# Output projection of 14 of 16 blocks: eight quarter products replaced by seven products of sums, in a fused attention and gated-FFN kernel

## The chip, the cores and the metric

One core of one Trainium2 chip. The metric is device time in microseconds (us) of the whole program, best read from runs in the fast state. Engines are named as in the profile: PE is TensorE (matmuls), PEld its weight loads, DVE is VectorE, ACT is ScalarE, POOL is GpSimd, SP the queue that issues the output transfers.

## The reference, cut to what matters

```python
# attention with projected K and V, 8 batches x 8 heads x 1024 x 64 (all fp32)
k_proj = einsum('ks,bhsd->bhkd', E, k);  v_proj = einsum('ks,bhsd->bhkd', F, v)
attn_out = softmax(q @ k_proj.T / 8) @ v_proj
x = attn_out.transpose(0, 2, 1, 3).reshape(8192, 512)
# gated FFN, d_model 512, d_ff 1536
gate = 1 / (1 + exp(-(x @ w_gate)));  val = x @ w_val
out = (gate * val) @ w_out            # [8192, 1536] @ [1536, 512]
```

The last line is the output projection. The kernel handles 16 blocks of 512 tokens, two for each batch.

## The kernel before

Everything is laid out so that TensorE never rests. A gate step makes 128 of the 1536 hidden features of a block: four matmuls for the gate and four for the value (512 columns each), a tanh on ScalarE and one product on VectorE into `hT` (bf16, features on partitions). The projection of the block before is slotted in between, one tile of 128 tokens at a time. Attention of the next batch runs in the gaps of ScalarE, VectorE and GpSimd.

```python
KV = [sbuf(f"KV{i}", [P, H, S // P * DH], BF16) for i in range(3)]    # K and V, three buffers
rrow = sbuf("rrow", [P, 4, 512], FP32)                                # reciprocal rows
FB, AB = (0, 1, 2, 3), (4, 5, 6, 7)      # four PSUM banks for the FFN, four for attention

def mstep(blk, m):                       # a gate step: 8 matmuls of 512 columns
    pbs = {n: ffn.next() for n in "GV"}
    ...
    gate(blk, m, pbs["G"], pbs["V"])     # ACT: tanh; DVE: hT[blk % 2][:, m, :]

def oproj(blk, tt, pb, cols=((0, DM),)):                # 128 tokens of a block
    ...
        for m in range(NF):                              # 12 matmuls of 512 columns
            mm(pb, bank[pb][:, 0 : c1 - c0],
               hT[blk % 2][:, m, tt * P : (tt + 1) * P], wO[:, m, c0:c1], ...)
        dve(... o = 0.5 * bank ...)                      # eviction
        add("SP", ... out_v[blk // 2, t] <- o ...)
# schedule: after gate steps 2, 5, 8 and 11 of a block, one tile of the block before
gaps = {2: [0], 5: [1], 8: [2], 11: [3]}
```

(Cuts are marked with dots; block 0 and the last block have their four tiles in a row.)

The softmax here doesn't subtract the row's maximum and nothing guards it: scores larger than these inputs give would overflow.

## Time and profile before

| | before |
|---|---|
| median, before the prediction | 562.15 us (561.75 to 563.31, 3 runs) |
| TensorE busy | 550.6 of 559.7 us |
| VectorE / ScalarE busy | 257.0 / 199.6 us |
| TensorE's waits after the first load | 0.3 and 0.2 us |

How to read it: with one engine at 98%, no waits and a chain of work that stays on it, the shares of the other engines matter only where they could be late. The time can fall by giving TensorE less to do. The lines stand in the prediction.

### The profile page before, as it was taken

What the parts mean: (1) busy time and instruction counts of PE and PEld (TensorE: products, weight loads), DVE (VectorE), ACT (ScalarE), POOL (GpSimd) and SP (SyncE); (2) the same over time, 40 slices, a digit from 0 to 9 for tenths busy, and PEclk for the clock granted to TensorE, in tenths of its full rate; (3) what the DMA queues carried; (4) which work ended last, traced back from release to release, by engine and by line L of the source; (5) the groups of instructions that cost most, each with busy time, mean ns of one, the idle gap of its engine ahead of it and who ended that gap; (6) DMA issues with size and microseconds to landing.
All of it is one profiled execution on the core that took longest, in us unless ns stands there. A gap on an engine that the chain in (4) does not pass through costs nothing.

```text
span 559.7 us, 7742 instructions
## 1 busy us (share of the span) xinstructions
PE 550.6 (98%) x3057; PEld 249.4 (45%) x3057; DVE 257.0 (46%) x397; ACT 199.6 (36%) x358; POOL 113.2 (20%) x148
## 2 busy tenths in 40 slices
PE   5999999999999999999999999999999999999998
PEld 4544444444444444444444444444444444444444
DVE  4645363235733564344733456335553357433332
ACT  3563813533253422533226422345224422222220
POOL 9210201003700270004500063000900026000000
DMA  9999997924491359105591158802401101110012
GB/s 176 198 200 195 174 224 156 202 68 95 92 215 45 76 100 213 50 27 117 101 191 38 29 115 133 168 20 49 102 32 38 39 22 39 37 39 31 26 37 95
DMA packets 76564, 56.01 MB, mean 100 GB/s; under 512 B 34704, under 2 KB 68240, under 8 KB 76528
## 3 DMA queue, kind: packets, MB, share of 16 engines
q0 software_dynamic: 33984, 29.89, 34.5%
q1 hardware_dynamic: 42544, 25.63, 17.4%
q8 instruction: 24, 0.39, 0.3%
q14 instruction: 12, 0.10, 0.1%
HBM read 60.29 MB, written 16.78 MB: 138 GB/s over the span
## 4 chain that ended last, share of the span: by engine, by line
PE 98%; DMA 1%; DVE 1%; ACT 0%; issue 0%; SPq 0%
PE pF L221 92%; PE pA L221 6%; DMA EF<-in_F_dram 1%; DVE rden L596 0%; DVE xT L645 0%; DVE hT L1056 0%; ACT qT L225 0%; SPq L307 0%; DVE vpD L498 0%; DVE ost L1087 0%; ACT kp L225 0%
## 5 line engine op out<-in xcount | busy, mean ns | idle before, releaser
L225 ACT ACTIVATE sig<-pF 128x512 f32<-128x512 f32 x192 | 115.6, 602 | 297.2 <-PE pF L221 289.8
L1056 DVE SCALAR_TENSOR_TENSOR hT<-sig,pF 128x512 bf16<-128x512 f32 x192 | 131.6, 686 | 167.9 <-PE pF L221 129.4
L221 PE MATMUL pF<-xT,wV 128*128 128x512 bf16 x768 | 197.9, 379 | 0.3 <-DVE hT L1056 0.3
L221 PE MATMUL pF<-xT,wG 128*128 128x512 bf16 x768 | 198.0, 379 | 0.1
L221 PE MATMUL pF<-wO,hT 128*128 128x512 bf16 (+1 forms) x780 | 175.3, 376 | 0.0
L890 POOL PARTITION_BROADCAST rb<-rrow x96 | 76.9, 862 | 287.0 <-DMA rrow<-rden 281.9
L221 PEld LDWEIGHTS pF<-wO,hT 128*128 128x128 bf16 x780 | 75.3, 98 | 91.1 <-issue 2.5
L221 PEld LDWEIGHTS pF<-xT,wV 128*128 128x128 bf16 x768 | 75.0, 98 | 90.9 <-DVE hT L1056 1.0
L221 PEld LDWEIGHTS pF<-xT,wG 128*128 128x128 bf16 x768 | 73.0, 98 | 93.8 <-issue 7.1
L1087 DVE TENSOR_SCALAR ost<-pF 128x512 f32<-128x512 f32 (+1 forms) x65 | 44.4, 684 | 109.4 <-PE pF L221 109.4
L920 DVE TENSOR_TENSOR xT<-xu,rb 128x512 bf16<-128x512 f32 x48 | 39.2, 858 | 0.0
L816 DVE RECIPROCAL rden<-pA 128x128 f32<-128x128 f32 x26 | 24.6, 950 | 12.7 <-PE pA L221 12.7
L225 ACT ACTIVATE xu<-pA 128x512 f32<-128x512 f32 x46 | 24.5, 616 | 1.1 <-PE pA L221 1.1
L225 ACT ACTIVATE eT<-pF 128x512 bf16<-128x512 f32 x29 | 15.8, 595 | 22.9 <-PE pF L221 22.7
L225 ACT ACTIVATE eT<-pA 128x512 bf16<-128x512 f32 x35 | 19.3, 625 | 1.0 <-PE pA L221 1.0
L221 PE MATMUL pA<-KV,EFT 128*64 128x512 bf16 (+2 forms) x168 | 15.5, 323 | 0.0
L239 POOL DMA_DIRECT2D KV<-in_k_dram x9 | 8.0, 885 | 34.4 <-PE pF L221 34.4
L239 POOL DMA_DIRECT2D Qb<-in_q_dram x11 | 9.4, 865 | 14.7 <-PE pF L221 14.7
L221 PEld LDWEIGHTS pA<-KV,EFT 128*64 128x64 bf16 x168 | 8.0, 109 | 6.9 <-issue 2.9
L225 ACT ACTIVATE vpD<-pA 64x512 bf16<-64x512 f32 (+2 forms) x20 | 9.7, 485 | 1.0 <-PE pA L221 0.5
L225 ACT ACTIVATE xu<-pF 128x512 f32<-128x512 f32 x14 | 7.6, 594 | 3.7 <-PE pF L221 3.7
L221 PE MATMUL pA<-eT,vpD 64*64 64x512 bf16 (+1 forms) x112 | 8.4, 351 | 0.0
(78 smaller groups left out, 119.4 us busy)
## 6 DMA issues: line engine op xcount, KB each, us to landing
out_dram<-ost SPq DMA_DIRECT2D x63, 256.0 KB, 2.0
Qb<-in_q_dram POOLq DMA_DIRECT2D x7, 1024.0 KB, 19.8
KV<-in_k_dram POOLq DMA_DIRECT2D x7, 1024.0 KB, 9.8
KV<-in_v_dram POOLq DMA_DIRECT2D x7, 1024.0 KB, 14.9
wO<-in_moe_w_out_dram POOLq DMA_DIRECT2D x1, 1536.0 KB, 12.5
wG<-in_moe_w_gate_dram POOLq DMA_DIRECT2D x5, 256.0 KB, 17.7
wV<-in_moe_w_val_dram POOLq DMA_DIRECT2D x5, 256.0 KB, 18.3
KV<-in_k_dram POOLq DMA_DIRECT2D x2, 512.0 KB, 7.2
```

The source lines that it names most:

```text
L221: return add("PE", lambda e: e.matmul(o, lhsT, rhs, **kw), r=r, x=[("bank", b)])
L225: return add("ACT", lambda e: e.activation(o, i, func, scale=scale), r=r, w=w, x=x)
L239: add("POOL", lambda e: e.dma_start(o, i), r=r, w=w, dma=sem)
L816: lambda e: e.reciprocal(rden[:, cc], bank[bk][:, cc]),
L890: lambda e, n=n, i=2 * rnd + c, j=j, parts=parts: e.partition_broadcast(rb[0:parts, n, :], rrow[32 * j : 32 * j + 1, i, :], channels=parts),
L920: lambda e: e.tensor_tensor(xT[s][:, r, :, 256 * g : 256 * g + 256], xu[:, n, :].rearrange("p (f c) -> p f c", f=2), y.rearrange("p (f c) ...
L1056: lambda e: e.scalar_tensor_tensor(hT[blk % 2][:, m, :], sg[:, :], 1.0, bank[pv][:, :], ALU.add, ALU.mult,),
L1087: lambda e, pb=pb, c0=c0, c1=c1: e.tensor_scalar(o[:, c0:c1], bank[pb][:, 0 : c1 - c0], 0.5, None, op0=ALU.mult),
```

## The change

A block's projection is A·B, with A the tokens by features and B the weights. Cut both into quarters: the token halves and feature halves of A, the feature halves and column halves of B. Four result quarters need eight quarter products. Winograd's form of Strassen's scheme needs seven, with sums: S1 = A21 + A22, S2 = S1 - A11, S3 = A11 - A21, S4 = A12 - S2 of the activations, and T1 to T4 of the weights, made once. The sums after the products are made in PSUM: one bank runs P1, then P1 + S2·T2, then + S3·T3, then + A22·T4; on the way ScalarE takes a snapshot three times, and VectorE adds a snapshot when it evicts the other bank.

```diff
+        def s_sums(blk, n, ms):                       # n = 1..4, three feature tiles at a time
+            o, a, b, op, r, w = {
+                1: (S1, A21, A22, ALU.add, "A21 A22", "S1"),
+                2: (S2, S1, A11, ALU.subtract, "S1 A11", "S2"),
+                3: (A21, A11, A21, ALU.subtract, "A11 A21", "A21"),    # in place
+                4: (A12, A12, S2, ALU.subtract, "A12 S2", "A12"),      # in place
+            }[n]
+            dve(lambda e: e.tensor_tensor(o, a, b, op), ...)
+        def first_products(blk):
+            a, c = ffn.next(), ffn.next()
+            product(blk, a, "A11", "B11", True)       # 12 matmuls of 256 columns
+            keep_snap(0, a)                           # ACT reads bank a
+            product(blk, c, "A12", "B21", True, True)
+            add_snap(0, c, 0, 0)                      # DVE: bank c + snapshot -> out tile
+            for ms in ((0, 3), (3, 6)):
+                s_sums(blk, 4, ms)
+            product(blk, a, "S2", "T2")
+            keep_snap(1, a)
+            product(blk, c, "S1", "T1", True)
+            product(blk, a, "A21", "T3")
+            keep_snap(2, a)
+            add_snap(2, c, 1, 1)
+        def last_products(blk):
+            product(blk, a, "A22", "T4", stop=True)
+            act(o, bank[a] ..., scale=0.5)
+            product(blk, c, "A12", "B22", stop=True)
+            add_snap(1, c, 0, 1)
 ...
-                    gaps = {2: [0], 5: [1], 8: [2], 11: [3]}
+                    if blk >= 2 and m[-1] == 3:
+                        todo.append(lambda blk=blk: first_products(blk - 1))
+                    if blk >= 2 and m[-1] == 4:
+                        todo.append(lambda blk=blk: last_products(blk - 1))
 ...
-        KV = [... for i in range(3)]
+        KV = [... for i in range(2)]
-        rrow = sbuf("rrow", [P, 4, 512], FP32)
+        rrow = (eT[:, :, :] ... .bitcast(FP32) ...)   # room for the sums: rows now lie over eT
 ...
-                spots = (3, 4, 6, 7, 12, 13, 14, 15, 15, 21, 23, 25, 27)
+                spots = (7, 8, 10, 11, 13, 14, 15, 16, 16, 20, 22, 24, 25)   # attention's places
```

The first three sums of a block stand behind its gate steps 9 to 11 and behind steps 0 to 2 of the next block; the fourth stands among the products. Below, a round is the work between one batch's first score matmuls and the next one's, two blocks long; the odd block is the second of a batch, in which the next batch's attention puts most of its work on VectorE. One gate step (step 4) stands between the fifth and the sixth product.

More of the change, by code (lines that the diff above doesn't have):

```diff
@@ L160, in bass_linformer_attn__then__ffn_glu_sigmoid_kernel @@
         Qb = sbuf("Qb", [P, H, S // P * DH], BF16)
-        KV = [sbuf(f"KV{i}", [P, H, S // P * DH], BF16) for i in range(3)]
+        KV = [sbuf(f"KV{i}", [P, H, S // P * DH], BF16) for i in range(2)]
         kp = sbuf("kp", [P, NR, DH], BF16)
@@ L170, in bass_linformer_attn__then__ffn_glu_sigmoid_kernel @@
         rhl = sbuf("rhl", [P, 512], BF16)
-        rrow = sbuf("rrow", [P, 4, 512], FP32)
+        rrow = (
+            eT[:, :, :].rearrange("p n c -> p (n c)").bitcast(FP32)
+            .rearrange("p (i c) -> p i c", i=4)
+        )
         rb = sbuf("rb", [P, 8, 512], FP32)
@@ L180, in bass_linformer_attn__then__ffn_glu_sigmoid_kernel @@
         hT = [sbuf(f"hT{i}", [P, NF, 512], BF16) for i in range(2)]
-        ost = [sbuf(f"ost{i}", [P, DM], FP32) for i in range(4)]
+        ost = sbuf("ost", [P, 4, DM], FP32)
+        wT = sbuf("wT", [P, 4, NF // 2, 256], BF16)
+        hS = sbuf("hS", [P, 2, NF // 2, 256], BF16)
+        snap = [EF[:, 0:512], EF[:, 512:1024], sbuf("snap2", [P, 512], FP32)[:, :]]
         bank = [
@@ L211, in bass_linformer_attn__then__ffn_glu_sigmoid_kernel, with mm @@
         ffn, att = Ring(FB), Ring(AB)
-        def mm(b, o, lhsT, rhs, r, start=True, stop=True, tp=None, tr=False):
-            kw = {}
+        def mm(b, o, lhsT, rhs, r, start=True, stop=True, tp=None, tr=False, read=False):
+            kw = {"skip_group_check": True} if read else {}
             if tp is not None:
@@ L244, in load_k @@
         def load_k(b):
-            n = 2 * b % 3
+            n = 0
             load(
@@ L254, in load_v @@
         def load_v(b):
-            n = (2 * b + 1) % 3
+            n = 1
             load(
@@ L710, in kv @@
                 for w in range(2):
-                    n = (2 * b + w) % 3
+                    n = w
                     src = KV[n][:, :, :].rearrange("p h (t d) -> p t h d", t=NT)
@@ L761, in k_alone @@
                 bk = att.next()
-                project(2 * b % 3, 0, [bk, bk], 0)
+                project(0, 0, [bk, bk], 0)
                 keep_k(bk, 0)
@@ L766, in v_alone @@
                 bk = att.next()
-                project((2 * b + 1) % 3, 1, [bk, bk], 0)
+                project(1, 1, [bk, bk], 0)
                 keep_v([bk, bk], 0, ["ACT"] * 4)
@@ L880, in gather @@
                         r=[("rden", c, R) for c in range(4) for R in range(2)],
-                        w=[("rrow", i)],
+                        w=[("rrow", i)] + [("eT", 2 * i + x) for x in range(2)],
                         dma=f"rrow{i}",
@@ L892, in spread @@
                             ),
-                            r=[("rrow", 2 * rnd + c)],
+                            r=[("rrow", 2 * rnd + c)]
+                            + [("eT", 4 * rnd + 2 * c + x) for x in range(2)],
                             w=[("rb", n)],
@@ L1064, in gate @@
                 [("sig", M % 3)],
-                [("hT", blk % 2, m)],
+                [("hT", blk % 2, m, n) for n in range(2)],
                 b=pv,
@@ L1069, in oproj @@
         def oproj(blk, tt, pb, cols=((0, DM),)):
-            T = 4 * blk + tt
-            o = ost[T % 4]
+            o = ost[:, tt, :]
             t = 2 * (2 * (blk % 2) + tt % 2) + tt // 2
@@ L1081, in oproj @@
                         wO[:, m, c0:c1],
-                        [("hT", blk % 2, m), "wO"],
+                        [("hT", blk % 2, m, tt // 2), "wO"],
                         start=(m == 0),
@@ L1090, in oproj @@
                     [],
-                    [("ost", T % 4, n)],
+                    [("ost", tt, x) for x in ((0, 1) if len(cols) == 1 else (n,))],
                     b=pb,
@@ L1096, in oproj, with t_sums @@
                     lambda e, c0=c0, c1=c1: e.dma_start(out_v[blk // 2, t][:, c0:c1], o[:, c0:c1]),
-                    r=[("ost", T % 4, n)],
-                    dma=f"out{T % 4}" if n == 0 else "outlast",
+                    r=[("ost", tt, x) for x in ((0, 1) if len(cols) == 1 else (n,))],
+                    dma=f"out{tt}" if n == 0 else "outlast",
+                )
+        H6 = NF // 2
+        def t_sums(n):
+            B11, B12 = wO[:, 0:H6, 0:256], wO[:, 0:H6, 256:512]
+            B21, B22 = wO[:, H6:NF, 0:256], wO[:, H6:NF, 256:512]
+            T = [wT[:, i, :, :] for i in range(4)]
+            a, b, op, r = (
+                (B12, B11, ALU.subtract, ["wO"]),
+                (B22, T[0], ALU.subtract, ["wO", ("wT", 0)]),
+                (B22, B12, ALU.subtract, ["wO"]),
+                (B21, T[1], ALU.subtract, ["wO", ("wT", 1)]),
+            )[n]
+            dve(lambda e: e.tensor_tensor(T[n], a, b, op), r, [("wT", n)])
@@ new lines, in s_sums @@
+        def s_sums(blk, n, ms):
+            h, (m0, m1) = hT[blk % 2], ms
+            lo, hi, up = slice(m0, m1), slice(H6 + m0, H6 + m1), range(m0, m1)
+            A11, A21 = h[:, lo, 0:256], h[:, lo, 256:512]
+            A12, A22 = h[:, hi, 0:256], h[:, hi, 256:512]
+            S1, S2 = hS[:, 0, lo, :], hS[:, 1, lo, :]
+            o, a, b, op, r, w = {
[4 more added lines that the diff above has]
+            }[n]
+            dve(
+                lambda e: e.tensor_tensor(o, a, b, op),
+                [k for x in r.split() for k in part(blk, x, up)],
+                [k for k in part(blk, w, up)],
+            )
@@ new lines, in part, with product @@
+        def part(blk, x, up):
+            if x[0] == "S":
+                return [(x, m) for m in up]
+            return [("hT", blk % 2, m + H6 * (x[2] == "2"), int(x[1]) - 1) for m in up]
+        def product(blk, bk, A, B, start=False, stop=False):
+            h = hT[blk % 2]
+            for j in range(2):
+                for m in range(H6):
+                    if A[0] == "S":
+                        lhsT = hS[:, int(A[1]) - 1, m, j * P : (j + 1) * P]
+                    else:
+                        c = 256 * (A[1] == "2") + j * P
+                        lhsT = h[:, m + H6 * (A[2] == "2"), c : c + P]
+                    if B[0] == "T":
+                        rhs, k = wT[:, int(B[1]) - 1, m, :], ("wT", int(B[1]) - 1)
+                    else:
+                        c = 256 * (B[2] == "2")
+                        rhs, k = wO[:, m + H6 * (B[1] == "2"), c : c + 256], "wO"
+                    mm(
+                        bk,
+                        bank[bk][:, 256 * j : 256 * j + 256],
+                        lhsT,
+                        rhs,
+                        part(blk, A, [m]) + [k],
+                        start=start and m == 0 and j == 0,
+                        stop=stop and m == H6 - 1 and j == 1,
+                        read=True,
+                    )
@@ new lines, in keep_snap, with quarter, add_snap @@
+        def keep_snap(n, bk):
+            act(snap[n], bank[bk][:, :], [], [("snap", n)], b=bk, scale=0.5)
+        def quarter(tok, col):
+            keys = [("ost", 2 * tok + j, col) for j in range(2)]
+            return ost[:, 2 * tok : 2 * tok + 2, 256 * col : 256 * col + 256], keys
+        def add_snap(n, bk, tok, col):
+            o, keys = quarter(tok, col)
+            dve(
+                lambda e: e.scalar_tensor_tensor(
+                    o,
+                    bank[bk][:, :].rearrange("p (j c) -> p j c", j=2),
+                    0.5,
+                    snap[n].rearrange("p (j c) -> p j c", j=2),
+                    ALU.mult,
+                    ALU.add,
+                ),
+                [("snap", n)],
+                keys,
+                b=bk,
+            )
@@ new lines, in bass_linformer_attn__then__ffn_glu_sigmoid_kernel @@
+        chain = []
+        def first_products(blk):
+            a, c = ffn.next(), ffn.next()
+            chain[:] = [a, c]
+            product(blk, a, "A11", "B11", True)
[10 more added lines that the diff above has]
+            add_snap(2, c, 1, 1)
@@ new lines, in last_products @@
+        def last_products(blk):
+            a, c = chain
+            product(blk, a, "A22", "T4", stop=True)
+            o, keys = quarter(1, 0)
+            act(o, bank[a][:, :].rearrange("p (j c) -> p j c", j=2), [], keys, b=a, scale=0.5)
+            product(blk, c, "A12", "B22", stop=True)
+            add_snap(1, c, 0, 1)
+            ffn.next(), ffn.next()
+            for tt in (2, 3, 0, 1):
+                t = 2 * (2 * (blk % 2) + tt % 2) + tt // 2
+                add(
+                    "SP",
+                    lambda e, tt=tt, t=t: e.dma_start(out_v[blk // 2, t], ost[:, tt, :]),
+                    r=[("ost", tt, n) for n in range(2)],
+                    dma=f"out{tt}",
@@ L1160, in second_loads, with sums @@
             pool(lambda e: e.load_library(spread_library))
+        def sums(blk, m):
+            if m >= 9 and 1 <= blk < 2 * B - 1:
+                s_sums(blk, m - 8, (0, 3))
+            if m <= 2 and blk >= 2:
+                s_sums(blk - 1, m + 1, (3, 6))
+            if blk == 2 and m <= 3:
+                t_sums(m)
         for b in range(B):
@@ L1167, in bass_linformer_attn__then__ffn_glu_sigmoid_kernel @@
                     ms = [[0, 1]] + ms[2:]
-                if blk == 1:
-                    gaps = {11: [0, 1, 2, 3]}
-                else:
-                    gaps = {2: [0], 5: [1], 8: [2], 11: [3]}
+                gaps = {11: [0, 1, 2, 3]} if blk == 1 else {}
                 for m in ms:
@@ L1177, in bass_linformer_attn__then__ffn_glu_sigmoid_kernel @@
                     else:
-                        todo.append(lambda blk=blk, m=m[0]: mstep(blk, m))
+                        todo.append(lambda blk=blk, m=m[0]: (mstep(blk, m), sums(blk, m)))
+                    if blk >= 2 and m[-1] == 3:
+                        todo.append(lambda blk=blk: first_products(blk - 1))
+                    if blk >= 2 and m[-1] == 4:
+                        todo.append(lambda blk=blk: last_products(blk - 1))
                     if blk >= 1:
@@ L1203, in bass_linformer_attn__then__ffn_glu_sigmoid_kernel @@
                 put(3, kv2)
-                spots = (8, 9, 11, 12, 17, 18, 19, 20, 20, 25, 27, 28, 30)
+                spots = (7, 8, 10, 11, 13, 14, 15, 16, 16, 20, 22, 24, 25)
             else:
-                spots = (3, 4, 6, 7, 12, 13, 14, 15, 15, 21, 23, 25, 27)
+                spots = (7, 8, 10, 11, 13, 14, 15, 16, 16, 20, 22, 24, 25)
             if b + 1 < B:
@@ L1220, in bass_linformer_attn__then__ffn_glu_sigmoid_kernel @@
                 put(4 if b == 1 else 1, lambda b=b: load_next(b + 2))
-                put(20 if b == 1 else 16, transpose_q)
+                put(16 if b == 1 else 14, transpose_q)
             for i, slot in enumerate(todo):
```

## The prediction

> **What bounds the kernel now.** I read the front page first (busy shares, then the chain that ended last), then the waits of TensorE, then its groups split by shape, then its timeline in one steady stretch. The page:
>
> ```profile
> PE 550.6 (98%) x3057; PEld 249.4 (45%) x3057; DVE 257.0 (46%) x397; ACT 199.6 (36%) x358; POOL 113.2 (20%) x148
> PE 98%; DMA 1%; DVE 1%; ACT 0%; issue 0%; SPq 0%
> ```
>
> TensorE (PE) is busy for 98% of the span and carries 98% of the chain that ended last. Busy does not yet mean productive, so the waits of TensorE come next. This is the whole list:
>
> ```profile
> PE pA L221 <- DMA EF<-in_F_dram: 5.6, 1, 5.6
> PE pF L221 <- DVE hT L1056: 0.3, 1, 0.3
> PE pA L221 <- ACT kp L225: 0.2, 1, 0.2
> ```
>
> Nothing after the first load costs more than 0.3 us, so no wait is there to be gained. Only less TensorE work shortens this kernel, and only if no new wait appears. The groups of TensorE by shape, and a stretch of its timeline (start, length, group):
>
> ```profile
> L221 PE MATMUL pF<-wO,hT 128*128 128x512 bf16 x756 | 172.7, 379 | 0.0
> L221 PE MATMUL pF<-wO,hT 128*128 128x384 bf16 x12 | 2.1, 326 | 0.0
> L221 PE MATMUL pF<-wO,hT 128*128 128x128 bf16 x12 | 0.8, 219 | 0.0
> ...
> 408.88 2.75 PE L221 MATMUL pF<-wO,hT 128*128 128x512 bf16 x12
> 411.47 1.03 PE L221 MATMUL pF<-xT,wG 128*128 128x512 bf16 x4
> 412.33 1.03 PE L221 MATMUL pF<-xT,wV 128*128 128x512 bf16 x4
> 413.20 1.03 PE L221 MATMUL pF<-xT,wG 128*128 128x512 bf16 x4
> ```
>
> The 379 ns of a row are its latency, not its pace. The pace comes from starts: from 408.88 to 411.47 twelve matmuls of 512 columns pass, 2.59 / 12 = 0.216 us each. At the very end stand 12 matmuls of 128 columns, each with a 128x128 weight load of its own: the group is 0.8 us long, less the last one's 0.219, over 11 steps, gives about 0.053 us (0.048 to 0.057 by the rounding). The 384-column group gives (2.1 - 0.326) / 11 = 0.161. So pace follows columns, and a fresh weight load per 128 columns did not slow it.
>
> **What the Trainium skill says.** "TensorE: Matmul & The Clock Gate", section "Back-to-back issue gap", gives N/2.4 + 2.5 ns warm, 518 cycles for 512 columns and 262 for 256. The trace agrees at 512 (216 ns) and at 128 (53 against 56). The same section names about 131 ns sustained for N=512 and 81 for N=128; the trace shows neither, so I use the formula. "VectorE: DVE Perf Modes", section "The perf-mode tier table", has tensor_tensor at two elements per cycle for bf16 in SBUF and at one with a PSUM operand; its measured (N+151)/0.96 gives 691 ns for 512, and the trace has 686 for the gate product. No bf16 tensor_tensor from SBUF stands in this trace. "SBUF — State Buffer", section "Who interferes with whom", says a VectorE instruction with two SBUF inputs contends with a GpSimd instruction that reads SBUF. The trace agrees: two xT products took 2.21 us while the broadcasts ran and 1.29 after. "PSUM — Partial Sum Buffer", section on bank collisions, forbids a matmul into a bank that ScalarE or VectorE reads; so each snapshot of a running sum is a true wait for TensorE.
>
> **The change part by part.** *Removed:* for 14 blocks, 48 matmuls of 512 columns, 48 x 0.2158 = 10.36 us of TensorE. *Added:* seven products of 12 matmuls of 256 columns (two token halves, six depth tiles), 84 x 0.1092 (262 cycles at 2.4 GHz) = 9.17 us. Saved 1.19 us a block, x 14 = **16.6 us**, all on the path, as TensorE never rests. Block 0 and the last block keep the old form, so the tail is unchanged.
>
> *VectorE:* removed 56 evictions at 0.69 = 38.7 us; added 42 evictions with a snapshot added at about 0.69 (one PSUM operand, as the gate product) = 29; 112 sums of 768 bf16 elements, estimated from the skill's formula at two per cycle as (384+151)/0.96 = 0.56 us = 62; four weight sums at 0.96 = 4. From 257 to about 313 us, 57% of the span. *ScalarE:* four reads of a bank per block, 56 x 0.6 = 34, to about 233 us, 43%. Neither becomes the bound on average; what matters is where they stand.
>
> *The tight place* is the run of five products between two steps of the next block. Both banks are read while the chain goes on. In the timeline VectorE starts about 0.27 us after the pace end of the last matmul of its bank (matmuls step to 411.47, the eviction starts at 411.74), and a matmul starts 0.06 us after the copy it waited for (VectorE's qT copy of 12.47 to 12.89, matmul at 12.95). The ScalarE snapshot of bank one needs 0.27 + 0.60 + 0.06 = 0.93 us while TensorE runs a product of 12 x 0.109 = 1.31 us in bank two; the VectorE eviction of bank two needs 0.27 + 0.69 + 0.06 = 1.02 us against 1.31. So each fits with 0.3 us to spare, if its engine is free.
>
> *Is VectorE free there?* The gate step has a period of 8 x 0.216 = 1.73 us. In the even block the first steps carry gate 0.69 + sum 0.56 = 1.25: free. In the odd block the reciprocals now stand in the same steps: 0.69 + 0.56 + 0.95 = 2.2 against 1.73, half a us behind per step over three steps. I put VectorE free some 1.9 us after the fourth step's end, while the first eviction is due 2.62 + 0.27 = 2.9 after it: fits. *Later in the odd block* eight xT products at 0.64, or 1.1 under the broadcasts, go after gates 4, 6, 8 and 9 with sums in between; each gate has some two steps (3.4 us) before its bank is wanted, and the worst I find by walking the queue leaves about 0.5 us.
>
> *Moved, hidden:* K and V lose the third buffer. The loads of a later batch are issued early in a round, and the K/V projection comes at its middle, some 30 us on (twelve gate steps, 20.7, and the products, 9.2); they land after 9.8 and 14.9 us, Q after 19.8. The buffers they fill were read in the round before. Reciprocal rows now lie over eT, whose readers are done by then, and whose next writer comes after the broadcasts (13.6 us). No cost expected.
>
> Sum: 562.15 - 16.6 = 545.6. I add 0.7 us for small gaps at bank changes: **546.3 us**.
>
> **Rivals.** *(1) Weight loads bound the short matmuls.* For: a load shows 98 ns, close to 109. Against: the 128-column group ran at 53 ns with one load each. That group is only 12 long and could have been queued in advance. Break-even is 10.36 / 84 = 0.123 us per step, only 25 ns above a load's own length; at that pace nothing is saved: 562. *(2) VectorE or ScalarE come late in the product chain.* For: margins of only 0.3 us, five bank turns per block, the odd block's load. If sums run at one element per cycle, (768+151)/0.96 = 0.96 us, the odd block falls another 1.2 us behind, and the first eviction comes about 0.3 us late; with the gates later in the odd block perhaps 0.5 to 1 us per odd block, 4 to 7 us in all: 550 to 553. *(3) A transfer is exposed by the two buffers.* For: Q is loaded last and its transposes now go ahead of the gather in SP's queue. Against: 20 us of load against 30 of slack. If wrong, some us per round for six rounds, 555 or more. *(4) Sums in bf16 cost nothing in time but accuracy;* not a matter of time.
>
> **Range and chances.** The pace of 256 columns is nearly certain by two bracketing shapes, so the saving lies at 15 to 18 us; the stalls are one-sided, 0 to about 8. That gives 543 to 553. Faster by over 2% means under 550.9 us, or stalls under 5.3 us, 0.38 a block: 0.77. Within 2%: 0.21, mostly rival 2. Slower: 0.02.
>
> **What would show it.** The 256-column group: 1176 matmuls with about 0.109 us between starts, that is 12 per 1.31 us in the timeline (rival 1: over 0.12). TensorE's waits: still no entry of a us or more in total outside the start; rival 2 shows as waits on snap, ost or hT inside the product chain, above all in odd blocks; rival 3 as waits on KV or qT transfers. The sums: 0.5 to 0.6 us each (0.9 to 1.0 if one element per cycle), longer under the broadcasts. VectorE busy near 313 us, ScalarE near 233. TensorE busy should fall by about 16 us with its share kept at 98%. I am wrong if the pace holds and the time does not fall: then a stall that I walked past in the queues is the cause.

## The result, and the profile after

The changed kernel took 547.4 us (median of 4 runs, 546.46 to 547.47) against 562.73 for the kernel before (4 runs, 561.75 to 563.83). The ratio is 0.9723, 95% interval 0.970 to 0.9746. Ratios here are the mean time of one kernel's fast runs over that of the other's of the same rounds, so not quite the ratio of the medians quoted. All outputs are right.

The page of the changed kernel, busy times and chain:

```profile
PE 530.7 (97%) x3504; PEld 298.7 (55%) x3561; DVE 305.5 (56%) x499; ACT 232.1 (43%) x414; POOL 113.5 (21%) x148
PE 93%; DMA 2%; DVE 1%; ACT 1%; issue 1%; POOL 1%; POOLq 0%
```

TensorE is still the bound. Its 3504 matmuls stand against 3561 weight loads: 57 matmul records are missing, so the 530.7 reads a little low. The 2% of DMA in the chain is one stretch of 12.6 us at the very start, the first V load; it is no new wait.

The whole list of TensorE's waits after the change:

```profile
PE pA L227 <- DMA EF<-in_F_dram: 5.8, 1, 5.8
PE pF L227 <- issue: 1.3, 8, 0.2
PE pA L227 <- DMA Qb<-in_q_dram: 0.4, 1, 0.4
PE pF L227 <- DVE hT L1063: 0.3, 1, 0.3
PE pA L227 <- DVE rhl L852: 0.3, 1, 0.3
PE pF L227 <- DMA KV<-in_k_dram: 0.3, 1, 0.3
PE pF L227 <- ACT EF L231: 0.3, 1, 0.3
PE pA L227 <- ACT kp L231: 0.2, 1, 0.2
```

The eight waits on "issue", 0.16 to 0.19 us each, stand where a group of four shows three records: a missing first matmul, not a wait. The waits on `Qb` and `KV` belong to the first 20 us. Two lines are new and real, and both outside the steady rounds: `rhl` (at 73 us, at the end of block 1) and `EF` (a snapshot buffer, at 96 us, in round 1), 0.3 us each. The timeline of TensorE over one block's products:

```profile
385.79 1.03 PE L227 MATMUL pF<-xT,wV 128*128 128x512 bf16 x4
386.66 2.78 PE L227 MATMUL pF<-wO,hT 128*128 128x256 bf16 x24
389.28 2.78 PE L227 MATMUL pF<-wT,hS 128*128 128x256 bf16 x24
391.90 1.47 PE L227 MATMUL pF<-wT,hT 128*128 128x256 bf16 x12
393.42 0.81 PE L227 MATMUL pF<-xT,wG 128*128 128x512 bf16 x3
394.07 1.03 PE L227 MATMUL pF<-xT,wV 128*128 128x512 bf16 x4
394.93 1.47 PE L227 MATMUL pF<-wT,hT 128*128 128x256 bf16 x12
396.24 1.47 PE L227 MATMUL pF<-wO,hT 128*128 128x256 bf16 x12
397.55 1.03 PE L227 MATMUL pF<-xT,wG 128*128 128x512 bf16 x4
```

From 386.66 to 389.28 two products of 12 matmuls pass: 2.62 / 24 = 0.109 us a matmul. The first five products follow one another without a gap, at 1.31 us each, and so do the last two behind the gate step. (Below, the pace end of a product is where the next matmul could start: its first start plus 1.31 us. The lengths shown run on to a modelled end, some 0.16 us later.) The same for VectorE in the odd block, its fullest place:

```profile
386.11 0.55 DVE L1138 TENSOR_TENSOR hT<-hT 128x768 bf16<-128x768 bf16 x1
386.57 0.95 DVE L822 RECIPROCAL rden<-pA 128x128 f32<-128x128 f32 x1
387.44 0.63 DVE L1063 SCALAR_TENSOR_TENSOR hT<-sig,pF 128x512 bf16<-128x512 f32 x1
389.58 0.69 DVE L1183 SCALAR_TENSOR_TENSOR ost<-pF,EF 128x512 f32<-128x512 f32 x1 [1.51 <-PE pF L227]
390.18 1.76 DVE L1138 TENSOR_TENSOR hT<-hT,hS 128x768 bf16<-128x768 bf16 x2
```

And two of its groups of sums (busy us, mean ns, idle before):

```profile
L1138 DVE TENSOR_TENSOR hT<-hT,hS 128x768 bf16<-128x768 bf16 x28 | 18.7, 708 | 0.0
L1138 DVE TENSOR_TENSOR hS<-hT 128x768 bf16<-128x768 bf16 x28 | 15.4, 551 | 0.0
```

VectorE is done with the last gate product at 388.07 and then sits idle for 1.51 us until TensorE gives it the first bank: in time, and with room. A sum takes 0.55 us. The fourth sum falls under the broadcasts of GpSimd in the odd blocks (0.88 each there) and has a mean of 0.71.

**Where the time went.** The start differs by up to 2 us from run to run (see "The total" below), so I count from the first score matmuls of batch 1 (512 columns) to the end of the last gate step. Timeline lines of TensorE, before:

```profile
57.97 0.41 PE L221 MATMUL pF<-qT,kpD 64*64 64x512 bf16 x4
...
543.93 13.14 PE L221 MATMUL pF<-wO,hT 128*128 128x512 bf16 x72
```

The 72 are the last tile of block 14 (12) and block 15 (60, of three widths), so the last gate step ended 12 x 0.2158 = 2.59 later, at 546.52: 488.55 us. After:

```profile
59.44 0.41 PE L227 MATMUL pF<-qT,kpD 64*64 64x512 bf16 x4
...
532.16 10.55 PE L227 MATMUL pF<-wO,hT 128*128 128x512 bf16 x59
```

Here the row is block 15 alone (59 of its 60 records are there), so the last gate step ended at 532.16: 472.72 us, or 15.83 less than before; predicted were 16.6 for the products alone. In the steady rounds the working was exact. The first score matmuls of two batches, before and then after:

```profile
360.13 0.41 PE L221 MATMUL pF<-qT,kpD 64*64 64x512 bf16 x4
...
427.10 0.41 PE L221 MATMUL pF<-qT,kpD 64*64 64x512 bf16 x4
```

```profile
364.67 0.41 PE L227 MATMUL pF<-qT,kpD 64*64 64x512 bf16 x4
...
429.26 0.41 PE L227 MATMUL pF<-qT,kpD 64*64 64x512 bf16 x4
```

A round takes 66.97 us before and 64.59 after, 2.38 less for two blocks, 1.19 a block. What is missing, 0.77, should stand in the two new waits, outside those rounds; their entries in the list, 0.3 each, are short because the modelled ends hide a part. The experiments take it up.

### The profile page after: what moved, and what is told of

Its sections match the earlier page's. It is cut to its first block, busy times and chain, and to the rows that moved or that the text cites. A ratio compares the mean times of both kernels' runs of the same rounds, so it can differ in the third digit from the quotient of the medians.

```text
span 545.4 us, 8923 instructions
## 1 busy us (share of the span) xinstructions
PE 530.7 (97%) x3504; PEld 298.7 (55%) x3561; DVE 305.5 (56%) x499; ACT 232.1 (43%) x414; POOL 113.5 (21%) x148
## 4 chain that ended last, share of the span: by engine, by line
PE 93%; DMA 2%; DVE 1%; ACT 1%; issue 1%; POOL 1%; POOLq 0%
PE pF L227 88%; PE pA L227 5%; DMA KV<-in_v_dram 2%; DVE hT L1063 0%; DVE rden L822 0%; POOL KV L245 0%; POOL Qb L245 0%; ACT xu L231 0%; ACT vpD L231 0%; ACT sig L231 0%; ACT eT L231 0%; ACT kpd L231 0%; DVE rden L602 0%; DVE hS L1138 0%; DVE xT L651 0%
## 5 line engine op out<-in xcount | busy, mean ns | idle before, releaser
L896 POOL PARTITION_BROADCAST rb<-eT x96 | 77.1, 864 | 279.6 <-DMA eT<-rden 274.5
L227 PE MATMUL pF<-wO,hT 128*128 128x256 bf16 (+3 forms) x610 | 80.8, 287 | 0.1
L227 PEld LDWEIGHTS pF<-wO,hT 128*128 128x128 bf16 x612 | 59.2, 98 | 19.7 <-issue 0.8
L1183 DVE SCALAR_TENSOR_TENSOR ost<-pF,EF 128x512 f32<-128x512 f32 x28 | 19.4, 692 | 51.4 <-PE pF L227 48.8
L227 PE MATMUL pF<-wT,hT 128*128 128x256 bf16 x336 | 41.2, 273 | 0.0
L227 PE MATMUL pF<-wT,hS 128*128 128x256 bf16 x336 | 39.0, 273 | 0.3 <-ACT EF L231 0.3
L231 ACT ACTIVATE EF<-pF 128x512 f32<-128x512 f32 x28 | 16.7, 597 | 47.0 <-PE pF L227 46.9
L227 PEld LDWEIGHTS pF<-wT,hT 128*128 128x128 bf16 x336 | 32.9, 98 | 6.8
L227 PEld LDWEIGHTS pF<-wT,hS 128*128 128x128 bf16 x336 | 32.8, 98 | 4.3 <-ACT EF L231 0.6
L1183 DVE SCALAR_TENSOR_TENSOR ost<-pF,snap 128x512 f32<-128x512 f32 x14 | 9.7, 692 | 35.6 <-PE pF L227 25.0
```

What stands on the lines that cost most here:

```text
L227: return add("PE", lambda e: e.matmul(o, lhsT, rhs, **kw), r=r, x=[("bank", b)])
L231: return add("ACT", lambda e: e.activation(o, i, func, scale=scale), r=r, w=w, x=x)
L896: lambda e, n=n, i=2 * rnd + c, j=j, parts=parts: e.partition_broadcast(rb[0:parts, n, :], rrow[32 * j : 32 * j + 1, i, :], channels=parts),
L1183: lambda e: e.scalar_tensor_tensor(o, bank[bk][:, :].rearrange("p (j c) -> p j c", j=2), 0.5, snap[n].rearrange("p (j c) -> p j c", j=2), ...
```

## The experiments

Ten runs: the changed kernel itself once more, and eight others, one of them twice. Times are medians; the kernel before had medians of 562.42 to 563.13 beside them. Where a time alone is too coarse, the text uses the stretch just defined, from the first scores of batch 1 to the end of the last gate step; the changed kernel, run again (a_again), had 532.68 - 59.96 = 472.72 us there, the same to 0.01.

**b_twobuf: the buffer part alone.** The kernel before, with two K and V buffers and the rows over `eT`, and nothing else of the change.

```diff
-        KV = [sbuf(f"KV{i}", ...) for i in range(3)]
+        KV = [sbuf(f"KV{i}", ...) for i in range(2)]
-        rrow = sbuf("rrow", [P, 4, 512], FP32)
+        rrow = (eT ... .bitcast(FP32) ...)      # with the dependencies on eT
```

> The kernel before with only the buffer part of the change: two K and V buffers instead of three, and the reciprocal rows laid over eT. Theory (transfers stay hidden): 562.7 us, ratio to before 0.998 to 1.002, no new wait of TensorE on KV or qT. Rival (a load that had gone ahead now has to wait for its buffer): one late load per round, some us for each of six rounds, 566 us or more, with TensorE waits on KV transfers.

Measured: 563.29 us, ratio 1.0002 (0.9987 to 1.0017). Between the same two places its timeline has 545.35 - 59.39 = 485.96 us, and the kernel before 543.93 - 57.97 = 485.96. No wait on a K or V transfer appeared. (One on Q, 0.4 us at 13 us, lies in the first loads.) The third buffer was worth nothing, and giving it up is free.

**a_eight: the new schedule with eight products.** Same banks, same places, 256-column products of the plain quarters, no sums, no snapshots.

```diff
+            product(blk, a, "A11", "B11", True)
+            product(blk, a, "A12", "B21", stop=True);  scale_out(a, 0, 0, "DVE")
+            product(blk, c, "A11", "B12", True)
+            product(blk, c, "A12", "B22", stop=True);  scale_out(c, 0, 1, "DVE")
+            product(blk, a, "A21", "B11", True)
+            product(blk, a, "A22", "B21", stop=True);  scale_out(a, 1, 0, "ACT")
+            ... gate step 4 ...
+            product(blk, c, "A21", "B12", True)
+            product(blk, c, "A22", "B22", stop=True);  scale_out(c, 1, 1, "DVE")
-            ... all calls of s_sums, t_sums, keep_snap and add_snap ...
```

> The changed kernel with its schedule kept (same banks, same places, 256-column products) but eight products of the plain quarters, no sums and no snapshots. Theory (the whole gain is the missing product): 12 matmuls more per block at 0.109 us, 14 blocks, 18.3 us over the changed kernel, 565 to 566 us, ratio to before 1.004 to 1.006. Rival (moving the projection into one place or sharing the evictions with ScalarE gives part of the gain): 560 us or less.

Measured: 565.04 us, ratio 1.0029 (1.0014 to 1.0044). The same two places in its timeline:

```profile
59.83 0.41 PE L227 MATMUL pF<-qT,kpD 64*64 64x512 bf16 x4
...
550.06 10.55 PE L227 MATMUL pF<-wO,hT 128*128 128x512 bf16 x59
```

That is 490.23 us, 17.51 over the changed kernel, for 14 x 12 = 168 matmuls more at 0.1092, which is 18.35; the missing 0.84 is what the two new waits of the changed kernel cost (a_tidy, below). The stretch is also 1.68 us longer than that of the kernel before: 96 matmuls of 256 columns take 96 x 0.1092 = 10.48 us, and the 48 of 512 took 10.36, which over 14 blocks makes 1.7. So the narrow products cost a little, and the rearrangement, ScalarE's share in the evictions and the new places of attention give nothing by themselves. The gain is the missing product.

**a_nogap: no gate step between the fifth and the sixth product.** The same instructions; step 4 comes after the seventh product. (Two calls that pass over two banks of the ring after the products go too, so that step 4 still gets the other two banks.)

```diff
+                    if blk >= 2 and m[-1] == 4:
+                        todo.append(lambda blk=blk: last_products(blk - 1))
                     todo.append(lambda blk=blk, m=m[0]: (mstep(blk, m), sums(blk, m)))
-                    if blk >= 2 and m[-1] == 4:
-                        todo.append(lambda blk=blk: last_products(blk - 1))
```

> The changed kernel with the gate step that stands between the fifth and the sixth product moved behind the seventh. The work is the same. Theory (a bank turn takes 0.27 us to the reader, 0.60 for the ScalarE snapshot and 0.06 back, 0.93 in all, and is hidden only when other work stands between): TensorE waits 0.93 us in each of 14 blocks for the third snapshot, 13 us more, 560.4 us, the wait shown as TensorE on ScalarE's snap. Rival (the reorder queue or later slack absorbs the wait): 547 to 549 us.

Measured: 558.7 us, ratio 0.9924 (0.9905 to 0.9944): 11.3 us lost of the 15.3 that the change gained. The first line of TensorE's waits:

```profile
PE pF L227 <- ACT snap L231: 9.6, 14, 0.7
```

One of the places in the timeline (lines of TensorE and of ScalarE; those of other engines are left out):

```profile
398.72 1.47 PE L227 MATMUL pF<-wT,hT 128*128 128x256 bf16 x12
400.23 0.60 ACT L231 ACTIVATE snap<-pF 128x512 f32<-128x512 f32 x1 [2.02 <-PE pF L227]
400.88 1.48 PE L227 MATMUL pF<-wT,hT 128*128 128x256 bf16 x12 [0.69 <-ACT snap L231]
```

Fourteen waits, one per block. The fifth product's pace ends at 398.72 + 1.31 = 400.03; ScalarE starts 0.20 later, reads for 0.60, and TensorE goes on 0.05 after that. The turn of a bank is 0.85 us here, not the 0.93 expected. Between the two fixed places the run takes 543.30 - 58.49 = 484.81 us, 12.09 more than the changed kernel, or 0.86 a block. The idle time shown, 0.69, is shorter because the profile counts a matmul as busy until its modelled end. The rival falls: the whole of the wait arrives in the time, and nothing absorbs it later.

**a_snap2 and a_snap2b: each snapshot read twice.** The first read goes to a spare tile.

```diff
         def keep_snap(n, bk):
+            act(dum[:, :], bank[bk][:, :], ["dum"], ["dum"], b=bk, scale=0.5)
             act(snap[n], bank[bk][:, :], [], [("snap", n)], b=bk, scale=0.5)
```

> The changed kernel with each snapshot's bank read twice by ScalarE (the first read goes to a spare buffer). Theory: the first two snapshots must fit into one product of 1.31 us; with a second read back to back (0.49 more) the turn is 0.27 + 0.60 + 0.49 + 0.06 = 1.42 us, 0.11 too long, 28 times, 3 us: 550.5 us, waits of TensorE on ScalarE only in the product chain. The third snapshot has a gate step to hide in and costs nothing. Rival A (the slack is larger than I think): 547.4. Rival B (ScalarE is already late there): over 556.

Measured: 550.39 us (median of the three fast runs; 550.85 with the slow one), ratio 0.9776 (0.976 to 0.9792). The profiled run was the slow one (566.43 us, granted clock 0.954), so its trace is not used. The same kernel again:

> The kernel with each snapshot read twice once more, because its profiled run fell in the slow state (granted clock 0.954) and shows no waits. A fast profile should place the 3.4 us that the fast runs showed: waits of TensorE on ScalarE's snapshot before the third and the fifth product, 28 of them at 0.10 to 0.15 us. The run without a gate step between showed the turn of a bank after a 256-column product to be 0.20 + 0.60 + 0.05 = 0.85 us; with a second read of 0.49 that is 1.34 against 1.31, which would give under 1 us in all; if the waits are that small, the rest of the 3.4 us lies elsewhere.

Measured: 549.94 us, ratio 0.9774 (0.976 to 0.9789). Its timeline:

```profile
390.92 2.79 PE L228 MATMUL pF<-wT,hS 128*128 128x256 bf16 x24
392.50 0.60 ACT L232 ACTIVATE dum<-pF 128x512 f32<-128x512 f32 x1 [1.64 <-PE pF L228]
392.99 0.59 ACT L232 ACTIVATE EF<-pF 128x512 f32<-128x512 f32 x1
393.64 1.48 PE L228 MATMUL pF<-wT,hT 128*128 128x256 bf16 x12
```

The third product's pace ends at 390.92 + 1.31 = 392.23. The reads run from 392.50 to 393.58, and TensorE starts the fifth product at 393.64: a turn of 1.41 us against 1.31, 0.10 too long. A round is 64.99 us (366.23 to 431.22) instead of 64.59, which is 0.10 for each of its four early snapshots, 2.8 us over 28. The expectation of the first submission (1.42, 3 us) was right. The second held two cases open; the 28 waits of 0.10 to 0.15 us came, and the turn of 1.34 with under 1 us did not: with the extra read, which carries a second wait of its own, the reader starts 0.27 us after the pace end and not 0.20; I argue that the second wait is the reason but did not test it. The waits hardly show in the list (one of 0.8 us, in round 1), because 0.10 is hidden under the modelled end of the last matmul; the round shows them. So the early snapshots have about 0.45 us to spare (1.31 less 0.85), no more.

**a_sums2 and a_sums3: each sum done two and three times.** The extra ones go to a spare tile.

```diff
-            dve(lambda e: e.tensor_tensor(o, a, b, op), ...)
+            for q, ws in ((dum[:, :, :], [("dum", 0)]), (o, part(blk, w, up))):    # a_sums3: dum twice, then o
+                dve(lambda e, q=q: e.tensor_tensor(q, a, b, op), ... + [("dum", 0)], ...)
```

> The changed kernel with each of the 112 sums of token halves done twice on VectorE (the first into a spare tile), some 0.5 us more each, which is a little more than if the sums ran at one element per cycle. VectorE busy should rise from 305 to about 365 us. My prediction put that case at 4 to 7 us (550 to 553, from stalls in the odd blocks); the trace of the changed kernel, where VectorE is done 1.4 us after the fourth gate step and the first eviction is due 2.9 us after it, now lets me expect less: 0 to 3 us, 547.4 to 550.5. Rival (VectorE is the hidden bound of the odd blocks): 1 us or more per odd block, 555 us or more.

Measured: 547.87 us, ratio 0.9733 (0.972 to 0.9746), VectorE busy 361.0 us. In the same rounds the changed kernel itself (a_again) had 547.37. The rounds are 64.59 us as before (365.05 to 429.63 is 64.58); past the first loads, the one change in TensorE's list is the wait on `rhl` in block 1, from 0.3 to 1.3 us. Between the two fixed places the run takes 532.53 - 58.82 = 473.71 us, 0.99 more than the changed kernel, which is just that wait; the 0.5 between the medians also carries the scatter of the start. VectorE has room for twice the sums everywhere but in block 1.

> The changed kernel with each of the 112 sums done three times. Doing them twice cost 0.5 us, of which 1.0 us more wait stood in block 1 alone. Theory (VectorE has slack until its backlog in the odd blocks passes the first eviction): three times adds another 0.5 us per sum step; in the odd block VectorE is then behind the first eviction by about 1.5 us, of which 0.3 to 0.5 is margin, so about 1 us for each of six odd blocks and 1 us in block 1 again: 554 to 557 us. Rival (slack is larger): under 550.

Measured: 579.42 us, ratio 1.0298 (1.027 to 1.0326), slower than the kernel before. Both my theory and its rival missed. (Three of its four runs show a granted clock of 0.997 in place of 1.0; 0.3% is under 2 of the 32 us lost.) The busy times of its page:

```profile
PE 541.7 (94%) x3504; PEld 295.3 (51%) x3561; DVE 427.4 (74%) x723; ACT 232.2 (40%) x414; POOL 120.5 (21%) x148
```

The two largest lines that grew or are new in TensorE's waits:

```profile
PE pF L228 <- DVE hT L1064: 13.6, 33, 0.8
PE pF L228 <- DVE ost L1185: 5.3, 7, 0.9
```

A round is 68.97 us (385.15 to 454.12), 4.4 more. I had looked only at the first eviction (`ost`, 5.3 us); the larger part is mostly in a place I had not walked: at the end of the odd block and the start of the next, each gate step carries a gate product and three sums, 2.25 us of VectorE (432.72 to 434.97) against a step of 1.73. There TensorE waits for `hT`, that is for the gate product to free its bank. VectorE is at 74% of the span on average when this happens: an average below 100% did not mean room.

**a_again, a_tidy and a_tidy15: the two waits taken away, and the last block too.** In a_tidy the sums of block 1 move from its last gate steps into the old projections that follow, and the K and V projection of round 1 comes one gate step earlier.

```diff
-            if m >= 9 and 1 <= blk < 2 * B - 1:
+            if m >= 9 and 2 <= blk < 2 * B - 1:
+                put(24, lambda: s_sums(1, 1, (0, 3)))
+                put(25, lambda: (s_sums(1, 2, (0, 3)), s_sums(1, 3, (0, 3))))
-                put(3, kv2)
+                put(2, kv2)
```

> The changed kernel as it is, for comparison with the next two on the same chip. 547.4 us, ratio to before 0.970 to 0.975.

> The changed kernel with two moves: the sums of block 1 go from its last three gate steps, where they delay the reciprocals that TensorE waits for (0.38 us), into the old projections that follow; and the K and V projection of round 1 goes one gate step earlier, so that ScalarE is free for the first snapshot (0.3 us). Theory: both waits vanish from TensorE's list, 0.7 us less than the changed kernel, 546.7. Rival (the time is taken back a little later, or the waits only move): within 0.2 us of the changed kernel.

Measured: the changed kernel again 547.37 us, ratio 0.9715 (0.9702 to 0.9728); tidied 545.92, ratio 0.9698 (0.9684 to 0.9711). The intervals overlap, so the time alone leaves it likely rather than sure. The trace decides: both waits are gone from TensorE's list, and these are the same two places in its timeline as above:

```profile
59.57 0.41 PE L227 MATMUL pF<-qT,kpD 64*64 64x512 bf16 x4
...
531.46 10.55 PE L227 MATMUL pF<-wO,hT 128*128 128x512 bf16 x59
```

471.89 us, 0.83 less than the changed kernel and 16.66 less than the kernel before. Counted from the same first scores, the matmul that had waited for `rhl` starts 0.39 us earlier (13.33 in place of 13.72), and the product that had waited for `EF` starts 0.82 earlier, 0.43 more. This is the predicted 16.6 in full, and a_eight stands 490.23 - 471.89 = 18.34 us above it, the 168 matmuls at 0.1092. It is also the fastest kernel.

In a_tidy15 block 15 uses seven products too, in the order that lets the last product of the second bank go first. (The transfers are cut from the diff.)

```diff
-        for tt in range(4):
-            oproj(last, tt, ffn.next(), ...)
+        for n in (1, 2, 3):
+            s_sums(last, n, (3, 6))
+        first_products(last)
+        product(last, c, "A12", "B22", stop=True);  add_snap(1, c, 0, 1)
+        product(last, a, "A22", "T4", stop=True);   act(ost ..., bank[a] ...)
```

> As the tidied kernel, and the last block's projection by seven products too. Theory: TensorE saves 1.19 us, but the last eviction is a whole bank of 512 columns and its transfer 256 KB in place of 64 KB, some 0.8 us later: 0.4 us less than the tidied kernel, 546.3. Rival (at the end nothing stands between the sums, the snapshots and the products, so each shows): 0.5 us or more over the tidied kernel.

Measured: 548.07 us, ratio 0.9731 (0.9718 to 0.9745), 2.15 over the tidied kernel. The rival holds. Its timelines put 0.5 of that at the start, which varies (first scores at 60.09 against 59.57 us), and 1.3 behind the last gate step (546.5 - 531.99 against 544.7 - 531.46). One line of the waits says where a part of it comes from:

```profile
PE pF L227 <- DVE ost L1183: 1.4, 1, 1.4
```

I had counted on bank two being free after its eviction; but that eviction adds the third snapshot, so it waits for ScalarE first: product, ScalarE, VectorE, TensorE, all in a row with no gate step to hide in. Up to the modelled end the wait shows as 1.4; from the pace end of the fifth product (537.23 + 1.31 = 538.54) to the next start (540.11) it is 1.57. So TensorE ends 0.4 us later in place of 1.19 earlier. The other 0.9 stand behind the last product, with its whole-bank eviction and larger transfer, for which 0.8 had been expected. The old form is right for the last block.

## Why the prediction was right, point by point

**The pace of 256 columns and the saving.** Predicted 0.109 us; measured 2.62 / 24 = 0.109. Weight loads did not bound it (rival 1). The 1.19 us a block came out exactly in the steady rounds (2.38 for two), and a_eight shows that nothing else contributes.

**The 0.7 us "for small gaps at bank changes".** The size was right (0.77), the place wrong, so the right size was luck. There are no gaps at the bank changes of the steady rounds. The loss stood in block 1, where the sums push back the reciprocals, and in round 1, where ScalarE was busy with the projected K and V when the first snapshot was due. a_tidy removes both and shows it.

**The tight place.** Predicted 0.93 us for a snapshot and 1.02 for an eviction. The snapshot's turn measured 0.85 (0.20 + 0.60 + 0.05); the eviction starts 0.30 after the pace end (389.28 to 389.58), so 0.30 + 0.69 + 0.05 = 1.04. Both fit into 1.31, as said; a_snap2b shows the edge from the other side. That a matmul must not write a bank while it is read is what the prediction took from "PSUM — Partial Sum Buffer"; no run here tests it.

**VectorE and ScalarE.** Predicted about 313 and 233 us busy; measured 305.5 and 232.1. A sum was put at 0.56 us and measured 0.55. This confirms two elements per cycle for a bf16 tensor_tensor in SBUF, as "VectorE: DVE Perf Modes", section "The perf-mode tier table", has it. (The (N+151)/0.96 that the prediction used stands in the same page's section on the TRN2 errata, for fp32; halving its N for bf16 was the prediction's own step.) In a row the next instruction starts 0.46 to 0.47 after a sum (386.11 to 386.57), and the other two kinds overlap likewise: an odd-block step of gate product, sum and reciprocal took 1.88 (385.56 to 387.44), not 2.2. So VectorE's backlog was smaller than walked: free 1.41 us after the fourth step (386.66 to 388.07), not 1.9.

**Rival 2 was put too high.** I put sums at half the rate at 4 to 7 us. Doing each sum twice, a little more than that, cost 1.0 us between the fixed places, all of it in block 1 and none in the steady rounds. The mis-sized term is the walk through the odd block, which added full lengths where the instructions overlap; VectorE's true edge lies between twice and three times.

**Rival 3.** The buffers cost nothing (b_twobuf).

**The total.** Predicted 546.3 us; measured 547.4. The runs of "before" that the sum started from had a median of 562.15, those beside the changed kernel 562.73. The two waits took 0.8, and the rest is within the scatter of the start: the first scores of batch 1 stand between 57.97 and 60.09 us in the eleven fast traces, the profile of before had the earliest, and the changed kernel itself had 59.44 once and 59.96 once.

## What to carry to other kernels

When one engine never waits, as here, a change is worth the work it takes from that engine, provided that every hand-over of a buffer fits behind other work of that engine: work out the turn of each bank (reader's start, read, return) and put a product or a step of at least that length between. Averages of the helping engines say little; walk their queues through the fullest stretch, and do not forget the first and the last round, where the usual cover is missing. To measure small gains, compare two fixed places in the timelines rather than whole spans, which here carried 2 us of scatter from the start.

## What the Trainium skill lacked or had wrong

- "TensorE: Matmul & The Clock Gate", section "Back-to-back issue gap": the sustained figures there (about 131 ns for 512 columns, 81 for 128) do not hold here: 216 ns for 512, and about 53 for 128 (one row of 12 only), each matmul with its own weight load. The section's formula, which it gives for an isolated matmul, holds in these rows, and for 256 columns too (109 ns).
- "PSUM — Partial Sum Buffer", section "PSUM bank collisions raise a hardware error": it says that PSUM has to be guarded by semaphores, bank by bank, but not what the turn costs. Here, after the last 256-column matmul's slot, ScalarE starts 0.20 us and VectorE 0.30 us later, and a matmul follows 0.05 us after the read; 0.85 us in all for a 512-column ScalarE read. The skill has lengths of single instructions, but no page gives this sum.
- "SBUF — State Buffer", section "Who interferes with whom": confirmed in kind, but no size is given for a broadcast on GpSimd. Here two bf16 sums took 1.76 us under the broadcasts and 1.02 without.
